# Chunk attention and an ELU feed-forward on one Trainium2 core: the middle group's second product by seven products of halves, and a new order of work

## The chip, the cores and the metric

One core of one Trainium2 chip runs the whole program as one launch. The metric is device time in microseconds (us). Three timed runs of the kernel before gave 825.3, 826.36 and 824.99 us (median 825.3). The profile is of one further execution, whose span from the first to the last instruction is 822.1 us.

## The reference

q, k and v are 8 x 8 x 576 x 64 in float32 (batch, heads, tokens, head size). Attention is local: every chunk of 64 tokens attends to itself.

```
scores = (q_c @ k_c.T) / 8          # per batch, head and chunk of 64 tokens
attn   = softmax(scores)
x      = attn @ v_c                 # laid out as 4608 tokens x 512
h      = x @ w_in                   # 512 -> 2048, the first product
g      = where(h > 0, h, exp(min(h, 0)) - 1)
out    = g @ w_out                  # 2048 -> 512, the second product
```

## The kernel before

**Numbers.** Each float32 operand of the two large products is held as a high and a low part ("hi", "lo"; a cast on ACT and a subtraction that makes the low part, together called a split below). One product of two tiles is three matmuls, hi.hi, hi.lo and lo.hi (`three`, L440), each 128x128 weights against 512 columns.

**Blocks.** The 4608 tokens are 9 blocks of 512. Blocks 0 to 2 are computed plainly: for each of 16 feature tiles f, `hidden` (L449) makes 12 matmuls of the first product, `elu` (L464) turns the result into g and splits it, and `second_products` makes 12 matmuls of the second product into four PSUM tiles `o0` to `o3`. The third block also prepares what the groups need.

**Groups.** Blocks 3 to 8 are three groups of two blocks (s = 0, 1, 2; s = 1 is the middle group). Their first product goes by Strassen-like combinations of halves: eight pairs of feature tiles a group, and for each pair seven products p1 to p7 of six matmuls (42 where the plain way needs 48). p1, p6, p7, p4 add up in one PSUM tile `x_ps`, p2, p5, p3 in another, `y_ps`; between them ACT copies intermediate sums out (`keep`, L764, items c1 to c4) and DVE adds them to the other tile (`add`, L767, items d1 to d3). A product that writes a tile next waits for the c or d that still reads it. `elu_of` (L685) then makes g of both blocks.

**Second product, groups 0 and 1.** g of the first block is multiplied at once, three matmuls for each of four token tiles (items Q; eight a pair, 24 matmuls). g of the other block is kept in `g_kept` and split (item G, `split_kept`, L818) and multiplied after the pairs (`KEPT`, 64 Q, 192 matmuls). The results are copied out and stored as rows of 512 features.

**Second product, group 2.** It goes by seven products of halves: products 1 and 2 in the course of the pairs (four Q a pair, 12 matmuls); then, in the order of `TURNED`, products 6, 5, 7, 4 and 3, each eight times 6 matmuls with the combination of weights as operand. `Pair.combine` (L743) makes the differences of g, `turn_split` (L1219) splits each operand into a ring of slots, `evacuate` (L1189) copies, adds, transposes and stores the transposed sums. Weight combinations come from DRAM: `combination` (L580) adds and subtracts parts of w_out on POOL, splits them and writes them to `b_dram`, half of the columns in group 0 (for two pairs in group 1's KEPT part) and half in group 1; `load_b` (L613) reads one back eight products ahead.

**Attention.** Each tile of 128 tokens is taken in ten steps, in blocks 3 on as letters: q k (DVE transposes, L365), s (scores on PE), m (maximum), E (exp), z (sums), h and w (normalise and transpose), v (times V on PE), x (copy out). One tile is done in every pair of groups 0 and 1 and one more in each KEPT.

**Order.** The engines run their instructions in program order, and the program order is written out by hand in strings of items: `START`, `FIRST_BLOCK`, `SECOND_BLOCK`, `LATER`, `THIRD_BLOCK`, `FIRST_PAIR`, `PAIR`, `LAST`, `TURNED`, `KEPT`. All loads but two and most stores are issued from SP's queue.

Of the kernel before, what the change touches and what calls it, by code (L numbers as in the profile page):

```python
# [21 lines left out]
def kernel(  # L22
# [19 lines left out]
    nc = tc.nc  # L42
# [18 lines left out]
    LAG = 1  # L61
    T2 = TB // 2
# [4 lines left out]

    first = ctx.enter_context(tc.tile_pool(name="first", bufs=1, side="right"))
# [4 lines left out]
    at = ctx.enter_context(tc.tile_pool(name="at", bufs=1))  # L73
    dram = ctx.enter_context(tc.tile_pool(name="dram", bufs=1, space=bass.MemoryType.DRAM))
# [16 lines left out]
    def w_out_tiles(pool):  # L91
        return [pool.tile([P, NF // 2, DM], F32R, name=name) for name in ("wo_hi", "wo_lo")]
# [81 lines left out]

    def subtract_next():
        (hi, lo), w = merged.pop(0)
        nc.vector.tensor_tensor(out=lo, in0=w, in1=hi.bitcast(F32), op=ALU.subtract)
# [97 lines left out]
    def early_attention(tt: int, q_sb, k_sb, get_v, kT, at, a_pool, get_banks, put, by_head: bool,  # L275
# [44 lines left out]
        else:  # L320
# [9 lines left out]
        nc.vector.tensor_tensor(  # L330
            out=a_heads, in0=a_heads, in1=z.broadcast_to([P, 2, NK, C]), op=ALU.mult
        )
# [15 lines left out]
    class Later:  # L348


        def __init__(self, n: int):
            self.n = n

# [19 lines left out]
        def less_max(self):  # L373
            mx = sm.tile([P, 2, NK, 1], F32, name="mx")
            nc.vector.tensor_reduce(out=mx, in_=self.scores, axis=AX.X, op=ALU.max)
            nc.vector.tensor_tensor(
                out=self.scores, in0=self.scores, in1=mx.broadcast_to([P, 2, NK, C]),
                op=ALU.subtract)

        def exp(self):  # L380
            nc.scalar.activation(out=self.scores, in_=self.scores, func=AF.Exp, scale=SCALE)

        def sums(self):
            self.z = sm.tile([P, 2, NK, 1], F32, name="z")
# [5 lines left out]
        def turn_a(self):  # L390

# [8 lines left out]

        def swap(self):

            for c in range(2):
                for e in range(2):
                    to, of = [slice(c * C + i * Q, c * C + (i + 1) * Q) for i in (e, 1 - e)]
                    nc.vector.transpose(
                        out=turned[to, 1 - e].rearrange("p (j h) t -> p j h t", j=2),
# [56 lines left out]
    def elu(h, engine=nc.vector):  # L464
# [13 lines left out]
        engine.tensor_tensor(out=glo, in0=e, in1=ghi.bitcast(F32), op=ALU.subtract)  # L478
# [25 lines left out]
    def combine():  # L504


        def pool(out, a, b, op):
            nc.gpsimd.tensor_tensor(out=out, in0=a, in1=b, op=op)
# [25 lines left out]
        def split(g):  # L534
            st = place_of(g)
            nc.scalar.copy(out=st[:, 0].bitcast(F32R), in_=st[:, 1])
            nc.vector.tensor_tensor(
                out=st[:, 1].bitcast(F32R), in0=st[:, 1], in1=st[:, 0], op=ALU.subtract)
# [41 lines left out]
    def combination(g: int, m: int, in_place: bool):  # L580

        half, f = divmod(2 * g, NF // 2)
        whi, wlo = [flat(w).bitcast(F32)[:, f * DM:(f + 2) * DM].rearrange(
            "p (i m c) -> p i m c", i=4, m=NM)[:, :, m] for w in (weights[half][2], weights[0][3])]
        sums = quad if in_place or g % 2 else k_turned
        a11, a21, a12, a22 = [sums[:, i] for i in range(4)]

        def pool(out, a, b, op):
            nc.gpsimd.tensor_tensor(out=out, in0=a, in1=b, op=op)

        pool(sums, whi, wlo, ALU.add)
# [7 lines left out]
        hi, lo = (spare(), flat(sums).bitcast(F32R)) if in_place else g_tiles()  # L599
        nc.scalar.copy(out=hi, in_=flat(sums))  # L600
        yield
        nc.vector.tensor_tensor(out=lo, in0=flat(sums), in1=hi.bitcast(F32), op=ALU.subtract)
        yield
        for i, src in enumerate((hi, lo)):
            nc.sync.dma_start(
                out=b_dram[g, :, 3:, i, m * P:(m + 1) * P],
                in_=src.bitcast(F32).rearrange("p (i c) -> p i c", i=4))
        yield
# [4 lines left out]
    def load_b(j: int):  # L613
        i, g = b_order[j]
# [723 lines left out]
```

## Time and profile before

| what | value |
|---|---|
| timed runs | 825.3, 826.36, 824.99 us, median 825.3 |
| span of the profiled execution | 822.1 us |
| PE busy | 814.1 us of the span, 5814 matmuls |
| DVE, ACT, POOL busy | 618.6, 492.4, 186.8 us |
| data moved | 181.40 MB, mean 221 GB/s |

A busy time is the sum over an engine's instructions. Matmuls overlap, so the time of one matmul in a row of them is read from the distance of starts, not from its own duration. Stages, in us from the span's start: the first product of block 0 starts at 27.5; block 1 at 125; block 2 at 218; the pairs of group 0 at 315, their KEPT part 442 to 487; the pairs of group 1 to 616.5, their KEPT part to 660; the pairs of group 2 to about 766, then the turned products until 818.5.

### The profile page before, as it was taken

To read this page: it belongs to the slowest core of one execution; us is meant where nothing else is said; L and a number is where in the kernel's file an instruction comes from. 1 tells how busy PE (TensorE), PEld (TensorE's weight loads), DVE (VectorE), ACT (ScalarE), POOL (GpSimd) and SP (SyncE) were. 2 spreads that over 40 slices of the span, in tenths; PEclk is the share of its full clock that TensorE was granted. 3 is DMA by queue.
4 is the path that set the end of the run, shared out by engine and by line. 5 is a ranking of instruction groups with operands and counts; after the bars stand their busy time and mean duration, and the time that the engine had idled before them with its cause. 6 is when DMAs were issued, how large, how long until landed. Compare 5 with 4: busy or idle time off the path is not lost.

```text
span 822.1 us, 15689 instructions
## 1 busy us (share of the span) xinstructions
PE 814.1 (99%) x5814; PEld 668.2 (81%) x5814; DVE 618.6 (75%) x947; ACT 492.4 (60%) x884; POOL 186.8 (23%) x196
## 2 busy tenths in 40 slices
PE   8999999999999999999999999999999999999998
PEld 7778788888888888888888888888888888888887
DVE  5999997777886798788778856778868547777745
ACT  6999985445644356665657336665566356777532
POOL 0000005554211210333343543234325000000000
PEclk9999999999999999999999999999999999999999
DMA  9947966776798996699999667899866357664677
GB/s 277 277 165 214 296 183 168 223 225 205 221 283 231 286 284 185 182 265 308 257 274 272 162 166 224 224 281 296 241 189 204 112 186 204 191 193 137 185 198 155
DMA packets 212075, 181.40 MB, mean 221 GB/s; under 512 B 73760, under 2 KB 190496, under 8 KB 212000
## 3 DMA queue, kind: packets, MB, share of 16 engines
q1 hardware_dynamic: 205088, 179.09, 77.6%
q10 hardware_dynamic: 6912, 1.31, 0.8%
q8 instruction: 46, 0.75, 0.4%
q14 instruction: 29, 0.24, 0.1%
HBM read 140.51 MB, written 42.99 MB: 223 GB/s over the span
## 4 chain that ended last, share of the span: by engine, by line
PE 97%; ACT 2%; DVE 0%; issue 0%; DVEq 0%; ACTq 0%
PE o L443 47%; PE h L443 43%; PE ps_a L259 2%; PE ps_a L267 2%; PE h L460 1%; ACT a L315 1%; PE ps_a L860 0%; PE ps_a L284 0%; PE ps_a L288 0%; PE ps_a L251 0%; PE ps_a L243 0%; ACT st L134 0%; ACT qT L340 0%; PE ps_a L335 0%; ACT xhi L434 0%; DVE mx L305 0%
## 5 line engine op out<-in xcount | busy, mean ns | idle before, releaser
L443 PE MATMUL o<-wo_hi,ghi 128*128 128x512 f32 x352 | 138.8, 394 | 0.0
L443 PE MATMUL o<-wo_hi,glo 128*128 128x512 f32 x352 | 137.4, 390 | 0.0
L443 PE MATMUL o<-wo_lo,ghi 128*128 128x512 f32 x352 | 137.1, 390 | 0.0
L443 PE MATMUL h<-xhi,wi_hi 128*128 128x512 f32 x324 | 108.1, 394 | 0.0
L443 PE MATMUL h<-xlo,wi_hi 128*128 128x512 f32 x324 | 106.7, 389 | 0.0
L700 POOL TENSOR_TENSOR glo<-e,ghi 128x512 fp32r<-128x512 f32 x32 | 41.4, 1293 | 172.1 <-ACT ghi L698 147.7
L443 PEld LDWEIGHTS o<-wo_hi,glo 128*128 128x128 f32 x352 | 66.1, 188 | 14.9 <-DVE glo L478 1.0
L443 PEld LDWEIGHTS o<-wo_hi,ghi 128*128 128x128 f32 x352 | 66.1, 188 | 14.0
L443 PEld LDWEIGHTS o<-wo_lo,ghi 128*128 128x128 f32 x352 | 66.1, 188 | 13.2
L443 PE MATMUL h<-wi_lo,wi_hi 128*128 128x512 f32 x288 | 75.0, 396 | 0.0
L765 ACT COPY kept<-h 128x512 f32<-128x512 f32 x72 | 42.1, 585 | 54.7 <-PE h L443 54.7
L443 PE MATMUL h<-wo_lo,wi_hi 128*128 128x512 f32 x288 | 71.8, 389 | 0.0
L443 PEld LDWEIGHTS h<-xhi,wi_hi 128*128 128x128 f32 x324 | 60.7, 188 | 13.3 <-ACT kept L765 0.4
L443 PE MATMUL o<-wo_hi,wo_lo 128*128 128x512 f32 x240 | 71.0, 390 | 0.0
L443 PEld LDWEIGHTS h<-xlo,wi_hi 128*128 128x128 f32 x324 | 60.8, 188 | 12.2
L443 PE MATMUL h<-xhi,wi_lo 128*128 128x512 f32 x180 | 70.2, 390 | 0.0
L443 PEld LDWEIGHTS h<-wo_lo,wi_hi 128*128 128x128 f32 x288 | 54.1, 188 | 11.2
L690 ACT ACTIVATE e<-e 128x512 f32<-128x512 f32 x96 | 60.8, 633 | 3.1
L443 PEld LDWEIGHTS h<-wi_lo,wi_hi 128*128 128x128 f32 x288 | 53.0, 188 | 11.4
L443 PE MATMUL o<-wo_lo 128*128 128x512 f32 (+1 forms) x198 | 60.2, 383 | 0.0
L693 DVE SCALAR_TENSOR_TENSOR g_kept<-e,g_kept 128x512 f32<-128x512 f32 x48 | 33.6, 701 | 31.5 <-ACT e L690 31.4
L467 ACT ACTIVATE e<-h 128x512 f32<-128x512 f32 x48 | 28.8, 600 | 41.5 <-PE h L443 38.0
(177 smaller groups left out, 1594.4 us busy)
## 6 DMA issues: line engine op xcount, KB each, us to landing
wi_hi<-a_dram SPq DMA_DIRECT2D x168, 256.0 KB, 4.1
wo_lo<-lo_dram SPq DMA_DIRECT2D x36, 512.0 KB, 5.5
wo_lo<-b_dram SPq DMA_DIRECT2D x56, 256.0 KB, 3.0
kept<-in_q_dram SPq DMA_DIRECT2D x100, 128.0 KB, 4.3
kept<-in_k_dram SPq DMA_DIRECT2D x100, 128.0 KB, 4.3
st<-in_moe_w_in_dram SPq DMA_DIRECT2D x16, 512.0 KB, 4.7
st<-in_moe_w_out_dram SPq DMA_DIRECT2D x16, 512.0 KB, 6.0
v_sb<-in_v_dram SPq DMA_DIRECT2D x32, 256.0 KB, 6.0
```

The lines of the kernel that those rows point to most:

```text
L259: nc.tensor.matmul(scores[halves[c], j, hp, :], lhsT=qT[halves[j], hp, halves[c]], rhs=kT[halves[j], hp, halves[c]], start=True, stop=True,)
L267: nc.tensor.matmul(x_ps[halves[j], c, hp, :], lhsT=v_sb[halves[c], 2 * hp + j, :], rhs=aT[halves[c], :, j * NK + hp], start=True, stop=True,)
L315: nc.scalar.activation(out=a_heads[:, j, h, :], in_=scores[:, j, h, :], func=AF.Exp, scale=SCALE, bias=mx[:, j, h, :], accum_out=z[:, j, h ...
L443: nc.tensor.matmul(ps, lhsT=a, rhs=b, start=start, stop=stop, skip_group_check=onto)
L460: nc.tensor.matmul(h, lhsT=w[:, kt, :], rhs=x[:, kt, :], start=i == 0, stop=i == len(terms) - 1)
L467: nc.scalar.activation(out=e, in_=h, func=AF.Relu, scale=-1.0)
L690: nc.scalar.activation(out=e, in_=e, func=AF.Exp, scale=-1.0)
L693: nc.vector.scalar_tensor_tensor(out=to, in0=e, scalar=-1.0, in1=c, op0=ALU.add, op1=ALU.max)
L700: engine.tensor_tensor(out=lo, in0=e, in1=hi.bitcast(F32), op=ALU.subtract)
L765: nc.scalar.copy(out=c21 if i == 4 else self.kept[i - 1], in_=x_ps)
```

## The change

The middle group's second product takes the seven products too (336 matmuls where it had 384). Its KEPT part goes; in its place stands `MID_TURNED`, with products 6, 5, 7, 4, 3, forty operand splits, the evacuations and the preparation of the last group's operands. Both column halves of every weight combination are now made in group 0 (`combination` has two tiles x and y). All strings behind `START` are written anew, with one string for each feature tile or pair. An item that ends in "!" has its two-input subtraction or addition moved to the other engine, from DVE to POOL or back (`combine_two`). Tile 28 takes its exponentials head by head, as six early tiles do (`BY_HEAD`). The high parts of w_out lie in pools of their own, and group 1's raw g, later its ring and group 2's `t2`, take their place.

```diff
+    def combine_two(engine, out, in0, in1, op=ALU.subtract):
+        if swapped[0]:
+            engine = nc.vector if engine is nc.gpsimd else nc.gpsimd
+        engine.tensor_tensor(out=out, in0=in0, in1=in1, op=op)
...
-    def combination(g: int, m: int, in_place: bool):
+    def combination(g: int, x, y, hx, hy):
...
+        pool(x, whi[:, :DM], wlo[:, :DM], ALU.add)
+        yield
+        pool(y, whi[:, DM:], wlo[:, DM:], ALU.add)
         yield
         pool(a22, a21, a22, ALU.add)
         pool(a21, a11, a21, ALU.subtract)
...
         def combine(self, item: str):
...
+            if s < NS - 1:
+                for to, a, b, op in {"1": [(b11, b12, b11, ALU.subtract)], "3": [(b12, b22, b12, ALU.subtract)],
+                                     "4": [(b21, b21, b22, ALU.subtract), (b21, b21, b11, ALU.add)]}[item]:
+                    combine_two(nc.gpsimd, to, a, b, op)
+                return
...
+    def turn_split(splits, ready, engine=nc.vector):
...
+            ring = ringed[-1] if n >= 2 * NG else weights[1][3]
+            hi, lo = [ring[:, 2 * (n % 4) + j, :] for j in range(2)]
+            if i == 6:
+                src = gp.tile([P, TB], F32, name="e")
+                combine_two(nc.vector, src, g_place(2 * g + 1), raw_place(0, g))
...
+            nc.scalar.copy(out=hi, in_=src)
+            combine_two(engine, lo, src, hi.bitcast(F32))
...
-    PAIR = (
-        "b b b m p1 c1 4 E Q 4 z p2 d1 Q p6 c2 b h b 1 Q Q 1 w p5 1 b q 1 Q l p7 c3 d2 k Q Q 2 p4 "
-        "c4 2 Q 3 p3 d3 3 3 3 s v x V"
+    MID_PAIRS = (
...
+        "p1 5 p2 c1 k p6 d1 5 4 4 E p5 c2 p7 c3 z h l d2 q w t1 Q 1 5 Q p4 t4 p3 c4 Q 2 s 1 1 "
+        "v 1 3 d3 2 Q x l t3",
...
+    MID_TURNED = (
+        "Y 6 H! 6 6 6 Y Y Q Z Q H Z G a10 a11 H! 6 6 s10 G! s11 5 t1! G 6 6 G 5 G t3! G G G! "
+        "5 u21 G 5 t4 5 G H G 5 5 5 u20 7 G! H! xB21 7 7 7 yB11! G! 7 G H! 7 G H! yt1! 7 xt3 "
+        "G G 7 u30 u31 4 4 xT1 H H! 4 G G! 4 H 4 a31 4 4 H G! G! a30 3 3 yt2! 4 s30 3 G 3 H! "
+        "G 3 yt4! s31 H! xT4 G! R 3 s40 xT2 R xT3! yB22 s41"
+    )
...
-        "s20 a21 s21 W1a s41a W0 s40 W1b s41b"
+        "4 G! a30 G 4 3 3 3 G! G! G! G! G s31 G! s30 3 3 3 3 G! G! G! G! 3 W1a W0 s41a a20 "
+        "s20 a21 s21 s40 W1b s41b"
...
-                (nc.scalar if which > 1 and i % 2 else nc.sync).dma_start(
+                (nc.scalar if which > 1 and i % 2 and s == NS - 1 else nc.sync).dma_start(
```

## Rows read from the trace of the kernel before

**Rows 1.** The page: busy time by engine; TensorE's granted clock in 40 slices.
```profile
PE 814.1 (99%) x5814; PEld 668.2 (81%) x5814; DVE 618.6 (75%) x947; ACT 492.4 (60%) x884; POOL 186.8 (23%) x196
...
PEclk9999999999999999999999999999999999999999
```

**Rows 2.** Busy time by stretch: stretch, length, PE, PEld, DVE, ACT, POOL, clock, DMA.
```profile
40.00:125.00 85.00, 85.00 (x603) 68.47 (x594) 78.81 (x115) 80.03 (x173) 0.00 (x0) 1.00 0.72 215
...
315.00:441.90 126.90, 126.90 (x968) 103.72 (x966) 101.31 (x165) 79.09 (x135) 40.05 (x45) 1.00 0.92 246
...
487.00:616.50 129.50, 129.50 (x1009) 105.97 (x1008) 94.42 (x155) 77.45 (x134) 46.95 (x55) 1.00 0.85 239
...
660.40:766.00 105.60, 105.60 (x467) 87.47 (x466) 72.19 (x111) 73.43 (x124) 0.00 (x0) 1.00 0.61 180
766.00:818.50 52.50, 52.48 (x248) 43.78 (x246) 32.00 (x51) 20.65 (x37) 0.00 (x0) 1.00 0.75 195
```

**Rows 3.** Waits of PE over the span, the longest group: total us, times, longest.
```profile
PE ps_a L243 <- ACT qT L340: 2.4, 3, 0.9
```

**Rows 4.** Timeline in group 2's pairs: start, us, engine, line, tiles, count, idle before.
```profile
696.87 1.52 PE L443 MATMUL h<-xhi,wi_hi 128*128 128x512 f32 x6
...
698.23 1.52 PE L443 MATMUL h<-xlo,wi_hi 128*128 128x512 f32 x6
...
698.43 0.59 ACT L765 COPY c<-h 128x512 f32<-128x512 f32 x1
...
699.59 1.52 PE L443 MATMUL h<-wi_lo,wi_hi 128*128 128x512 f32 x6
...
699.79 0.69 DVE L769 TENSOR_TENSOR g_kept<-h,kept 128x512 f32<-128x512 f32 x1 [0.71 <-PE h L443]
```

**Rows 5.** Group 1's pairs, DVE alone: tile ps_a; L365; L769; L693.
```profile
487.00:616.50 129.50, 8.81 (x480) 7.72 (x480) 39.59 (x77) 8.13 (x14) 1.00 0.85 239
...
487.00:616.50 129.50, 13.10 (x12) 1.00 0.85 239
...
487.00:616.50 129.50, 16.12 (x24) 1.00 0.85 239
...
487.00:616.50 129.50, 20.87 (x30) 1.00 0.85 239
```

**Rows 6.** Groups of instructions: forms, count, busy us, mean ns, idle before.
```profile
L700 POOL TENSOR_TENSOR glo<-e,ghi 128x512 fp32r<-128x512 f32 x32 | 41.4, 1293 | 172.1 <-ACT ghi L698 147.7 <-PE h L443 17.7 <-DMA kept<-in_k_dram 6.7
...
L683 DVE TENSOR_TENSOR xf<-xf 128x1024 f32<-128x1024 f32 x8 | 11.1, 1389 | 0.1
...
L678 DVE TENSOR_TENSOR wi_lo<-xf,wi_lo 128x1024 fp32r<-128x1024 f32 x6 | 7.7, 1279 | 0.0
...
L1226 DVE TENSOR_TENSOR wi_lo<-g_kept,wi_lo 128x512 fp32r<-128x512 f32 x8 | 5.3, 687 | 4.3 <-ACT wi_lo L1225 4.3
...
L1225 ACT CAST wi_lo<-g_kept 128x512 fp32r<-128x512 f32 x8 | 4.8, 622 | 7.2 <-issue 5.0 <-DVE wi_lo L1226 1.5 <-DVE wo_lo L1226 0.7
...
L1211 DVE STREAM_TRANSPOSE c<-o 128x512 f32<-128x512 f32 x3 | 2.1, 716 | 3.7 <-PE o L443 3.7
```

**Rows 7.** Timeline of DVE in group 1's KEPT part.
```profile
620.15 1.82 DVE L700 TENSOR_TENSOR wo_lo<-g_kept,wo_lo 128x512 fp32r<-128x512 f32 x2 [2.93 <-ACT wo_lo L698]
...
623.10 2.54 DVE L700 TENSOR_TENSOR wo_lo<-g_kept,wo_lo 128x512 fp32r<-128x512 f32 x2
```

**Rows 8.** Timeline of POOL over the same time.
```profile
620.64 2.74 POOL L589 TENSOR_TENSOR k_turned<-k_turned 128x128 f32<-128x128 f32 x4
623.35 1.74 POOL L589 TENSOR_TENSOR quad<-wo_hi,wo_lo 128x512 f32<-128x512 f32 x1
```

**Rows 9.** Line L700: duration in ns, least, median and most, first and last start.
```profile
L700 DVE TENSOR_TENSOR wo_lo<-g_kept,wo_lo x13: 678/693/1786, 445.1 to 644.5; 128x512 fp32r<-128x512 f32 x13
```

**Rows 10.** DMA issues: count, KB each, median us from issue to landing.
```profile
wo_lo<-b_dram SPq DMA_DIRECT2D x56, 256.0 KB, 3.0
```

**Rows 11.** Timeline near the end: two stores' issues on SP; the last DVE instruction.
```profile
800.63 0.87 SPq L1214 DMA_DIRECT2D out_dram<-k_turned  x2
...
818.51 0.45 DVE L1211 STREAM_TRANSPOSE c<-o 128x256 f32<-128x256 f32 x1 [1.43 <-PE o L443]
```

More of the change, by code (lines that the diff above doesn't have):

```diff
@@ L61 @@
     LAG = 1
+    TURN = 1
     T2 = TB // 2
@@ L1157 @@
     for f in range(NF):
-        for item in THIRD_BLOCK.get(f, ODD if f % 2 else EVEN).split():
+        for item in items_of(BLOCK_THREE[f]):
             if item == "H":
@@ L1205, in evacuate @@
             if which == 2:
-                to = (turned, unturned)[m].rearrange("p e h t -> p (e h t)")
-            elif which == 3:
+                to = spares[m]
+            elif which == 3 and s == NS - 1:
                 to = k_flat if m == 0 else flat(at.tile([P, NK, P], F32, name="qT"))
@@ L1264 @@
-            for item in order.split():
-                if item[0] == "u":
-                    evacuate(item)
+            order = (PAIRS, MID_PAIRS, LAST_PAIRS)[s][g]
+            if not s and 2 <= g < NG - 1:
+                combining = combination(g, *sum_places(g))
+            for item in items_of(order):
+                if item[0] in "uas" and len(item) > 1:
+                    evacuate(item, s)
+                elif item[0] in "AS" and len(item) > 1:
+                    evacuate(item.lower(), s - 1)
+                elif item in "GH":
+                    turn_split(splits, ready, nc.gpsimd if item == "H" else nc.vector)
@@ L1267 @@
                 elif not pair_step(item, before):
                     do(item)
-        if last:
-            break
+        if s >= TURN:
+            done = {i: 0 for i in range(1, 8)}
+            for item in items_of((MID_TURNED, TURNED)[last]):
+                if item in "65743":
+                    i, g = int(item), done[int(item)]
+                    done[i] += 1
+                    for m in range(NM):
+                        b_product(s, i, g, m, *(t2_place(g) if i == 6 and last else ready[i, g]))
+                elif item == "R":
+                    for m in range(NM):
+                        queue.append((s, 3, done[3], m, *ready[3, done[3]]))
+                    done[3] += 1
+                elif item[0] == "W":
+                    for g in range(done[4], NG):
+                        b_product(s, 4, g, int(item[1]), *ready[4, g],
+                                  {"a": slice(T2), "b": slice(T2, TB)}.get(item[2:], slice(TB)))
+                elif item in "GH":
+                    turn_split(splits, ready, nc.gpsimd if item == "H" else nc.vector)
+                elif item == "Q":
+                    second_next()
+                elif item in "YZ":
+                    next(pair.parts["3" if item == "Y" else "4"])
+                elif item[0] in "uas":
+                    evacuate(item, s)
+                elif item[0] == "t":
+                    pair.combine(item[1])
+                else:
+                    do(item)
+            continue
@@ L1273 @@
         for row, line in enumerate(KEPT):
-            if s == NS - 2 and row == 0:
-                combining = chain(combination(0, 0, False), combination(1, 0, False))
-            for item in line.split():
+            if row == 0:
+                combining = chain(*[combination(g, *sum_places(g)) for g in (0, 1, NG - 1)])
+            for item in items_of(line):
                 if item == "4":
```

330 lines of the change are left out of this document (192 added, 138 removed), and 111 rows, old and new, of tables (BLOCK_THREE, BLOCK_TWO, FIRST_BLOCK, KEPT).

## The prediction

> **What bounds the kernel now.** I read the page's busy times first, then the stretches, then the waits of TensorE (PE), and last the timeline at a few places. PE is busy for 814.1 of 822.1 us, and its granted clock stands at the top digit in all 40 slices [rows 1]. In every stretch from 40 us on PE's busy time is the stretch itself (126.90 of 126.90, 129.50 of 129.50, 105.60 of 105.60) [rows 2]. A busy PE could still step slowly, so the step has to be read: six matmuls of 512 columns start 1.36 us after the six before them (696.87, 698.23, 699.59), which is 0.2267 us each [rows 4]. PE's longest group of waits is 2.4 us in all [rows 3], and since PE is busy without a gap behind 40 us, it lies in the start. So from 27.5 us to the last matmul the time is the number of matmuls times their step, and only two things can change it: fewer matmuls, or waits that aren't there today.
>
> The other engines are below PE: DVE 101.3 of 126.9 in group 0's pairs (80%), 94.4 of 129.5 in group 1's (73%), 72.2 of 105.6 in group 2's [rows 2].
>
> **What is removed.** The middle group's second product takes 2 blocks x 16 feature tiles x 4 token tiles x 3 = 384 matmuls. By seven products it takes 7 x 8 pairs x 2 column halves x 3 = 336, 96 of them for products 1 and 2 in the pairs and 240 for the other five behind them. 48 matmuls go, 48 x 0.2267 = 10.9 us [rows 4]. All have 512 columns, as the ones that go. I counted the other matmuls in the strings: first products, attention tiles and the number of changes between large and small matmuls (16 in block 0, four in block 1) are as before. The start string is the same, so the first large matmul stays at 27.5 us.
>
> **What is added beside PE, middle group's pairs.** The stretch now holds 38 Q where it had 64, so 26 x 3 x 0.2267 = 17.7 us less: 129.5 - 17.7 = 111.8 us. DVE's work in it today is attention 39.6 + 13.1, the additions d1 to d3 16.1, and ELU's last step 20.9 [rows 5]; 94.4 less these leaves 4.7 for the weight combinations' splits, which move to group 0. New on DVE are 13 subtractions that "!" puts there, 13 x 0.687 = 8.9 [rows 6]. Sum: 39.6 + 13.1 + 16.1 + 20.9 + 8.9 = 98.6 of 111.8 us, 88%. POOL has 12 splits, 20 differences of g and 4 parts of the first turned operands, 36 x 1.293 = 46.5 us [rows 6]. ACT loses eight casts (8 x 0.622 = 5.0): 72.5 of 111.8 [rows 2, 6]. Tile 28's exponentials head by head turn one ACT instruction into sixteen short ones, in one pair; the third of ACT that is free covers them.
>
> **Turned part of the middle group.** 38 products of 6 and two Q: 234 matmuls, 53.0 us, against 192 matmuls (43.5) in the part that goes. DVE: 24 low parts and 7 other subtractions at 0.687 (21.3), four additions at about 0.69 (2.8), six transposes at 0.716 (4.3), and for the last group's operands five of 1.279 and four of 1.389 (12.0): 40.4 of 53.0 us, 76% [rows 6]. ACT: 37 casts at 0.622 (23.0), seven of twice the size, at most twice that (8.7), and eight copies and ELU steps, estimated at a cast each (5.0): 36.7 of 53. POOL: 18 x 1.293 and two of twice the size, 28.5 us. All are under PE. They need an order in which each comes in time, and group 2 has such an order today: PE 52.48 of 52.50 us with DVE at 61% [rows 2].
>
> **Group 0.** Its pairs keep their length. On DVE come four more splits of combinations (2.7) and about seven moved subtractions and additions more than leave (4.8), from 101.3 to about 109 of 126.9; with a few transferred preparations at most 112, 88%. POOL goes from 40 to about 50. Each combination now writes 1 MB in the group where it wrote half of that: 5 x 0.5 MB more in 127 us on a mean of 246 GB/s, 8% more traffic [rows 2]. The loads of operands are issued a whole pair (16 us) ahead, so I take nothing for it.
>
> **SP's queue.** The middle group's stores all go through SP now: 32 at 0.44 us each [rows 11], 14 us of issue in 53, in order with 40 weight loads. A weight load is issued eight products ahead (8 x 1.36 = 10.9 us) and lands 3.0 us after issue [rows 10], so a store that waits for its transpose may hold it back by some 7 us before PE sees it. Cost: nothing; if a transpose came over 7 us late, what it is late by.
>
> **Moved in block 0 to 2 and in the last group.** No PE wait is there to be won, so there is nothing below zero; what hides the new order is that block 0 runs without a PE wait at DVE 78.8 and ACT 80.0 of 85.0 us [rows 2]. In the tail two pairs of stores fall behind the product of whole columns instead of ahead of it; the last instruction is the same half transpose [rows 11]: 0 to +1 us, I take 0.
>
> **Waits that the new order may add.** Today c copies are covered by one product (1.36 us) in group 2, and d additions by at least 2.04 (p, Q). By my count of the new strings 15 of 69 hand-offs through DVE are left with one product. ACT's copy and DVE's addition both start 0.20 us after the last matmul's successor has started and take 0.59 and 0.69 [rows 4]; a covered d has 1.36 - 0.89 = 0.47 us to spare. An instruction of DVE ahead of it takes up to 1.09 (13.10 over 12) [rows 5], so the worst is 0.62 late, 15 x 0.62 = 9.3 us; the least is 0, as in block 0. Behind a late d stands PE's next product, and PE has nothing else. The nearest row is block 0, with DVE at 93% and no wait, so I take 1.0 us, keep 0 and 9.3 for the range.
>
> **The sum.** 822.1 - 10.9 + 1.0 = 812.2 us of span. The runs' median lies 3.2 us above the profiled span, which I carry over: **815.4 us**.
>
> **A shared way to memory.** POOL and DVE disturb each other: two DVE subtractions with both inputs in SBUF took 1.82 us beside POOL's additions, two more 2.54 [rows 7, 8], where the median is 0.693 and the most 1.786 [rows 9]. That is 4.36 - 4 x 0.69 = 1.6 us over for four, 0.40 each. The change puts POOL to work all through the group. The Trainium skill (SBUF — State Buffer, "Who interferes with whom") says that a VectorE instruction with two SBUF inputs and a GpSimd instruction that reads SBUF exclude each other for the whole instruction. The rows agree with it in kind; the sum by it would be rival A's, 819.
>
> **Rivals.**
>
> A: in the turned part POOL's instructions and DVE's with two SBUF inputs run one at a time. Two-input work in it is 21.3 + 12.0 = 33.3 us on DVE and 28.5 on POOL, 61.8 in 53.0. Two double-sized POOL subtractions (5.2) may run on below the last group's first pair: 56.6, 3.6 us over: 815.4 + 3.6 = 819.0. For it: rows 7 and 9. Against it: in group 1's KEPT part PE lost nothing to these; part of each instruction may overlap, and the first splits run ahead.
>
> B: the hand-offs cost their worst, 9.3 instead of 1.0: 823.7, no change to be measured. Against it: DVE would have to be behind each time.
>
> C, slower: DVE becomes the bound of the pairs. If each two-input subtraction or ELU step there waits for POOL: 43 in the middle pairs, some 45 in group 0's, 39 in the turned part. DVE's room is 111.8 - 98.6 = 13.2, 15 and 12.6 us. At a mean delay p the overrun is 127p - 41 us: nothing below 0.32 us, 9.8 us at 0.40, and over the gain and the bound of measurement (10.9 + 1.7) from 0.42 on. At 0.45, 16.2 us: 814.4 + 16.2 = 830.6. For it: 0.40 for four instructions in the rows. Against it: these all met POOL, and POOL is busy 42% of the middle pairs, which makes a mean nearer to 0.2.
>
> D: the matmuls aren't saved. The strings hold 336, so I give it nothing.
>
> **Numbers.** What a measurement here can tell from no change is 0.2%, 1.7 us. Forecast (813.2 to 817.5) 0.70; A and its like (up to 821.5) 0.16; B 0.06; C 0.08. The forecast and A are faster, B is the same, C slower: 0.86, 0.06, 0.08. The range 813.2 to 821.5 holds the first two.
>
> **What would show it.** PE with 5766 matmuls, busy in all of every stretch behind 27.5 us; the middle pairs 112 us long with DVE near 99, the turned part 53. A PE wait on an addition of L767's kind would show B; subtractions of over 1 us beside POOL, and PE waiting on low parts in the turned part, A; the same in the pairs, with DVE at the stretch's length, C. The forecast is wrong if PE's waits behind 27.5 us sum to more than 3 us.

## The result, and the profile after

The changed kernel takes 831.5 us (median of 4 runs, 830.4 to 833.1) against 825.5 beside it: ratio 1.0074, 95% interval 1.0060 to 1.0089. It is slower, where 815.4 was forecast and 821.5 was the end of the range. The profiled execution took 833.1 us, the longest of the four, and its span is 831.3. So the places below account for the 9.2 us between two profiled spans, where the medians differ by 6.0.

First the page of the changed kernel, for [rows 1]: busy time, TensorE's granted clock, the traffic, and the chain that ended last.
```profile
PE 811.3 (98%) x5766; PEld 660.3 (79%) x5766; DVE 628.1 (76%) x917; ACT 507.1 (61%) x925; POOL 348.6 (42%) x267
...
PEclk9999999999999999999999999999999999999999
...
DMA packets 225390, 187.72 MB, mean 226 GB/s; under 512 B 91168, under 2 KB 199712, under 8 KB 225312
...
PE 81%; DVE 8%; ACT 5%; DMA 3%; issue 2%; SPq 1%; POOL 0%; DVEq 0%; ACTq 0%; POOLq 0%
```
The chain on the page before:
```profile
PE 97%; ACT 2%; DVE 0%; issue 0%; DVEq 0%; ACTq 0%
```
The 48 matmuls are gone (5766 for 5814). POOL has nearly twice its work. In the chain 19% is now something other than PE's work; before it was 3%.

The stretches, for [rows 2] (same columns): block 0, group 0's pairs, the middle pairs, the turned part, the last pairs, the tail.
```profile
40.00:125.00 85.00, 83.27 (x551) 65.97 (x549) 77.35 (x92) 76.89 (x168) 31.43 (x20) 1.00 0.73 214
316.10:443.00 126.90, 126.71 (x908) 103.56 (x908) 104.72 (x168) 79.14 (x136) 49.89 (x43) 1.00 0.89 251
493.70:615.60 121.90, 115.01 (x929) 91.82 (x928) 100.17 (x160) 77.96 (x136) 57.77 (x41) 0.99 0.82 230
615.60:670.40 54.80, 54.41 (x237) 44.02 (x236) 43.46 (x52) 32.27 (x52) 24.69 (x17) 1.00 0.75 200
670.40:776.00 105.60, 104.53 (x460) 85.79 (x459) 66.39 (x92) 72.17 (x126) 37.02 (x25) 1.00 0.67 187
776.00:827.50 51.50, 51.49 (x243) 43.02 (x241) 22.30 (x29) 20.32 (x35) 29.28 (x21) 1.00 0.78 194
```
The middle pairs take 121.9 us, not 111.8, with DVE at 100.2 (82%), not far from the 98.6 forecast: the work was counted rightly, the time wasn't. PE stands still for 6.9 us in them and for 1.7 in block 0, where it had stood for none.

The waits of PE behind its first large matmul: us in total, times, longest.
```profile
PE h L492 <- DVE c L835: 2.8, 3, 2.4
PE h L492 <- DMA wi_hi<-a_dram: 2.5, 1, 2.5
PE h L492 <- ACT kept L831: 1.2, 2, 0.9
PE h L492 <- DVE e L519: 1.1, 1, 1.1
PE ps_a L279 <- DVE turned L455: 1.0, 1, 1.0
PE o L492 <- DVE kept L532: 0.8, 1, 0.8
```
No single cause stands out in this view, and the engine named is the last in a row of causes. I took all starts of large matmuls and added up what each came later than its step of 0.2267 us: 16.8 us behind the first large matmul, where it was 0.16 before. By place: blocks 0 to 2 2.8, group 0 and KEPT 3.2 (with 0.9 at 496.8 and 498.3 us, where KEPT's last products alternate with the first middle pair), middle pairs 8.5, turned part 0.9, last pairs 1.4. The sum of the span: 822.1 - 10.9 + 16.8 - 0.2 + 1.1 (the first large matmul starts at 28.6, not 27.5) + 2.2 (single steps longer by up to 0.12 us, and 0.4 near the end) is 831.1, and 831.3 was measured.

**The two longest waits go back to SP.** SP's issues and the matmul that waited, in the middle pairs:
```profile
514.60 5.98 SPq L243 DMA_DIRECT2D kept<-in_q_dram  x8
...
520.62 5.32 SPq L243 DMA_DIRECT2D kept<-in_k_dram  x8
...
526.04 1.83 SPq L705 DMA_DIRECT2D wi_hi<-a_dram  x3
...
529.39 2.98 PE L492 MATMUL h<-wo_lo,wi_hi 128*128 128x512 f32 x12 [2.49 <-DMA wi_hi<-a_dram]
```
Tile 31 lies across two batches and needs sixteen loads. SP issues them in one row for 11.3 us; the weight operand of product 6 stands behind them, is issued at 526.04 at the earliest and comes 2.5 us late. Before, the same sixteen went out in one row too, with no wait of PE:
```profile
513.21 4.19 SPq L223 DMA_DIRECT2D kept<-in_q_dram  x8
517.44 4.83 SPq L223 DMA_DIRECT2D kept<-in_k_dram  x8
522.37 1.18 SPq L643 DMA_DIRECT2D wi_hi<-a_dram  x2
```
So it isn't the row by itself that costs, but how soon PE needs what stands behind it. Some 30 us on, the same queue is late for tile 33:
```profile
551.56 1.97 SPq L243 DMA_DIRECT2D kept<-in_q_dram  x4
...
558.34 1.08 DVE L384 STREAM_TRANSPOSE qT<-kept 128x512 f32<-128x512 f32 x1 [4.04 <-DMA kept<-in_q_dram]
...
561.18 0.68 DVE L835 TENSOR_TENSOR c<-h,kept 128x512 f32<-128x512 f32 x1
...
561.91 2.06 PE L492 MATMUL h<-wo_lo,wi_hi 128*128 128x512 f32 x6 [2.36 <-DVE c L835]
...
563.77 2.75 PE L492 MATMUL h<-t_place,wi_hi 128*128 128x512 f32 x6
```
The wait is put down to DVE, but DVE had itself waited 4.04 us for q of tile 33, whose load SP issued only at 551.56, with the pair's first sum queued behind. Six matmuls then take 2.75 us where they took 1.52: in 562.2 to 566.3 us the granted clock is 0.59, near the lower level (1.2 of 2.4 GHz), after a PE that had stood still for 2.4 us. By the steps that adds 1.6 us to the 2.5.

The operands of the second product land later as well, here in 500 to 612 us, for [rows 10], whose median was 3.0 us (all 56 of those loads were the last group's, so the place differs too):
```profile
wo_lo<-b_dram SPq DMA_DIRECT2D x18, 256.0 KB, 4.8
```

**Block 0.** DVE, POOL and PE around the first wait:
```profile
36.60 1.69 DVE L162 TENSOR_SCALAR st<-st 128x1024 f32<-128x1024 f32 x1
...
37.70 1.74 POOL L193 TENSOR_TENSOR wi_lo<-xf,wi_hi 128x512 fp32r<-128x512 f32 x1
38.21 1.78 DVE L193 TENSOR_TENSOR wo_lo<-xf,wo_hi 128x512 fp32r<-128x512 f32 x1
...
42.58 0.50 PE L492 MATMUL h<-xhi,wi_hi 128*128 128x512 f32 x1 [1.07 <-DVE e L519]
```
A subtraction of 0.69 us takes 1.78 beside POOL's, and what stands behind it on DVE comes late for PE. Over the whole run DVE's longer instructions take some 50 us more than the medians of their forms, against some 10 before; 16 of these lie in the first 125 us, where before had 0.2.

**The last pairs.** The first sum into c waits for the middle group's stores out of c:
```profile
677.07 0.69 DVE L835 TENSOR_TENSOR c<-h,kept 128x512 f32<-128x512 f32 x1 [2.06 <-DMA out_dram<-c]
```

### The profile page after: what moved, and what is told of

It is laid out like the page before. It is cut to its first block, busy times and chain, and to the rows that moved or that the text cites. A ratio compares the mean times of both kernels' runs of the same rounds, so it can differ in the third digit from the quotient of the medians.

```text
span 831.3 us, 15888 instructions
## 1 busy us (share of the span) xinstructions
PE 811.3 (98%) x5766; PEld 660.3 (79%) x5766; DVE 628.1 (76%) x917; ACT 507.1 (61%) x925; POOL 348.6 (42%) x267
## 4 chain that ended last, share of the span: by engine, by line
PE 81%; DVE 8%; ACT 5%; DMA 3%; issue 2%; SPq 1%; POOL 0%; DVEq 0%; ACTq 0%; POOLq 0%
PE o L492 39%; PE h L492 36%; PE ps_a L279 2%; PE ps_a L287 1%; DMA wi_hi<-a_dram 1%; ACT st L140 1%; DVE wo_lo L193 1%; ACT st L145 1%; DVE xf L169 1%; DMA b_dram<-unturned 1%; PE h L509 1%; DMA kept<-in_q_dram 1%; ACT a L335 1%; DVE xf L173 1%; DVE turned L455 1%
## 5 line engine op out<-in xcount | busy, mean ns | idle before, releaser
L193 POOL TENSOR_TENSOR glo<-e,ghi 128x512 fp32r<-128x512 f32 x36 | 49.6, 1377 | 156.4 <-ACT ghi L524 111.8
L492 PE MATMUL o<-wo_hi,ghi 128*128 128x512 f32 x272 | 107.7, 396 | 0.0
L492 PE MATMUL o<-wo_hi,glo 128*128 128x512 f32 x272 | 106.3, 391 | 0.2 <-POOL glo L193 0.2
L492 PE MATMUL o<-wo_lo,ghi 128*128 128x512 f32 x272 | 106.0, 390 | 0.0
L492 PE MATMUL h<-wi_lo,wi_hi 128*128 128x512 f32 x288 | 70.3, 391 | 0.0
L492 PEld LDWEIGHTS o<-wo_hi,glo 128*128 128x128 f32 x272 | 51.1, 188 | 12.0 <-DVE glo L193 0.7
L492 PEld LDWEIGHTS o<-wo_hi,ghi 128*128 128x128 f32 x272 | 51.1, 188 | 11.0 <-ACT ghi L524 0.2
L492 PEld LDWEIGHTS o<-wo_lo,ghi 128*128 128x128 f32 x272 | 51.1, 188 | 10.2
L835 DVE TENSOR_TENSOR g_kept<-h,kept 128x512 f32<-128x512 f32 x48 | 33.1, 689 | 27.2 <-PE h L492 14.5
L492 PEld LDWEIGHTS o<-wo_lo 128*128 128x128 f32 x246 | 45.4, 188 | 10.3 <-DVE wo_lo L193 0.6
```

Of the source, the lines that this page charges most:

```text
L193: engine.tensor_tensor(out=out, in0=in0, in1=in1, op=op)
L492: nc.tensor.matmul(ps, lhsT=a, rhs=b, start=start, stop=stop, skip_group_check=onto)
L835: nc.vector.tensor_tensor(out=to, in0=y_ps, in1=self.kept[kept], op=ALU.add)
```

## The experiments

Each time stands beside the kernel before, 825.3 to 825.5 us in all sets.

| run | us | ratio to before, 95% |
|---|---|---|
| e1 old blocks | 831.6 | 1.0040 to 1.0116 |
| e2 no swaps | 861.9 | 1.0434 to 1.0468 |
| e3 loads moved | 828.3 | 1.0026 to 1.0060 |
| e4 POOL in before | 830.9 | 1.0055 to 1.0085 |
| e5 repaired | 827.2 | 1.0013 to 1.0035 |
| e6 new blocks | 829.3 | 1.0039 to 1.0062 |
| e8 spread | 828.0 | 1.0022 to 1.0049 |
| e9 quarter loads | 825.7 | 0.9999 to 1.0018 |
| e10 no turns | 827.6 | 1.0012 to 1.0039 |
| e11 best | 825.9 | 0.9993 to 1.0010 |
| e12 two queues | 832.5 | 1.0063 to 1.0121 |
| e13 places | 825.7 | 0.9996 to 1.0014 |
| e14 KEPT's end | 828.3 | 1.0020 to 1.0043 |
| e15 first block | 822.3 | 0.9946 to 0.9973 |

My theory after the result: the matmuls are saved in full, and the loss lies at single places with causes of their own (POOL beside DVE in block 0, SP's order, the stores out of c). The rival: DVE, at 88% of the middle pairs by the forecast, has no slack left, so that what is repaired in one place is paid for in the next.

**e1, blocks 0 to 2 as before**
```diff
-    FIRST_BLOCK, BLOCK_TWO, BLOCK_THREE of the changed kernel
+    FIRST_BLOCK, SECOND_BLOCK, LATER, THIRD_BLOCK of the kernel before
```


> The changed kernel with the orders of blocks 0, 1 and 2 as they were before (27 to 315 us of the trace). The changed kernel's PE waits in block 0 sum to 2.6 us, and its first large matmul starts 1.1 us later than before. If the new order of block 0 makes them (with 22 subtractions moved to POOL), both go: 831.5 - 2.6 to - 3.7, 828 to 829 us, and PE has no wait behind 28 us until 430 us. If PE's waits there are the chip's or memory placement's, the time stays within 1 us of 831.5. Either way the waits from 430 us on stay, some 14 us.

831.6 us, no gain. Block 0's waits are gone, but PE now waits 2.7 us at 321.5 us, with slow matmuls behind, in group 0's first pair: the older third block leaves ScalarE another backlog than the new pair was ordered for. What the blocks cost stayed open.

**e2, every "!" without effect**
```diff
-            swapped[0] = item[-1] == "!"
+            swapped[0] = False
```


> The changed kernel with every '!' without effect: each subtraction stays on the engine that it had. Theory 'shared reading' (POOL's instructions and DVE's with two SBUF inputs wait for each other): DVE's lengthened instructions in block 0, KEPT and the turned parts fall from 52 us in all to under 25, PE's waits in block 0 (2.6 us) and in KEPT (2.9 us) go, and the time falls by 3 to 6 us, to 825.5 to 828.5. Rival 'DVE is full': with 22 subtractions back on DVE in block 0 and a dozen in KEPT, DVE is late and the time rises, over 832. Theory 'SP's queue' expects the waits at 526 to 529 us and 559 to 566 us, some 6.5 us together with the slower clock behind them, to stay in either case.

861.9 us: PE's waits sum to 43 us. A "!" moves operations both ways (net, 51 more run on POOL with them: 267 instructions there, 216 without), and the rest of the order is built on it. So this run can't price POOL beside DVE; it shows that this order is worse without the moves.

**e3, tile 31's loads in two halves, tile 33's earlier**
```diff
-        ... "p4 1 c4 1 V 3 1 m p3 d3"          "p1 p2 5 E c1 l z 4 ... p7 Q Q 4 t1 ..."
+        ... "p4 1 c4 1 V 3 1 m p3 d3 j"        "p1 p2 5 E c1 z 4 ... p7 Q Q J 4 t1 ..."
-        ... "Q m 3 1! Q"                       "... c3 z h l d2 q w t1 ..."
+        ... "Q m 3 1! Q l"                     "... c3 z h d2 q w t1 ..."
```
(j issues tile 31's q, J its k.)

> The changed kernel with three loads of tokens moved in SP's queue, nothing else: tile 31's sixteen loads in two halves, eight at the end of the first middle pair and eight behind p7 of the second (were: sixteen together ahead of p6's operand of the next pair), and tile 33's eight at the end of the third middle pair (were: behind p7's operand in the fourth). Theory 'SP's queue': the wait of 2.5 us on p6's operand at 529 us and the wait of DVE (4.0 us) on tile 33 with PE's 2.4 us and the stretch at half clock behind it go: 831.5 - 5 to - 7, 824.5 to 826.5 us, granted clock back to 1.000 in most runs. Rival 'DVE is the bound of the middle pairs' (88% and waits): PE waits as long for DVE elsewhere in the same stretch, and the time stays over 829.

828.3 us, 3.2 less in the median and 6.6 in the profiled executions. The matmul that had waited 2.49 us for its operand, from the trace of this run:
```profile
526.47 1.65 PE L492 MATMUL h<-wo_lo,wi_hi 128*128 128x512 f32 x6 [0.15 <-DVE c L835]
```
The wait at 561.9 and the half clock are gone too; a new wait of 2.0 us comes at 534.7, where DVE turns tile 31's k before it has landed. SP's order is shown as a cause.

**e4, the kernel before with POOL in block 0**
```diff
-        nc.vector.tensor_tensor(
+        (nc.gpsimd if on_pool else nc.vector).tensor_tensor(
```
(22 of the first block's subtractions, those that the new string marks; nothing else differs from before.)

> The kernel before, in its own order, with 22 of block 0's subtractions on POOL, those that '!' marks in the changed kernel (13 low parts of weights, 9 of g). Theory 'shared reading': DVE's own work falls by 15 us but its instructions are lengthened by 8 us or more in block 0, POOL's subtractions are late, and PE, which had no wait there, gets waits of 1 to 6 us: 826.5 to 831.5. Rival 'only the new order costs': an engine with less work and the same order makes no wait: 825.5, within 0.5 us.

830.9 us, 5.6 slower by these moves alone. One of them, from its trace:
```profile
46.15 1.73 POOL L181 TENSOR_TENSOR wi_lo<-xf,wi_hi 128x512 fp32r<-128x512 f32 x1
46.66 2.37 DVE L181 TENSOR_TENSOR wo_lo<-xf,wo_hi 128x512 fp32r<-128x512 f32 x2
...
48.48 0.50 PE L447 MATMUL o<-wo_lo,ghi 128*128 128x512 f32 x1 [0.75 <-DVE wo_lo L181]
```
Two subtractions that remain on DVE take 2.37 us where they need 1.4, and PE waits for the second. Giving DVE less to do made DVE later.

**e7, the shared reading by itself**
```diff
+    for beside in (None, act, gp_two):
+        for on_vector in (vector_two, vector_bank, vector_one, vector_three, vector_turn):
+            barrier()
+            for i in range(12):
+                on_vector()
+                if beside and (beside is act or i < 6):
+                    beside()
```


> The shared reading measured by itself; no part of the computation is done. VectorE runs twelve instructions of one kind on 128x512 float32, five kinds in turn (subtraction of two SBUF tiles, of a PSUM and an SBUF tile, scalar addition of one SBUF tile, the scalar_tensor_tensor of two SBUF tiles, the transpose); first alone, then beside twelve ScalarE copies, then beside six GpSimd subtractions of two SBUF tiles; then six GpSimd subtractions run alone. Theory (VectorE and GpSimd read SBUF in turns, instruction by instruction): alone 0.69 us each (transpose 1.1); beside ScalarE the same; beside GpSimd a VectorE instruction that meets one takes 1.0 to 1.8 us, and the stretch of twelve is longer by 4 to 6 us, for the kinds with two SBUF inputs, and for the scalar addition too; the transpose and the one with a PSUM input less. Rival (only kinds with two SBUF inputs take turns): scalar addition, PSUM subtraction and transpose unchanged to within 5%.

Its timeline: start, us for all instructions of the row, engine, line, tiles, count. First VectorE alone (two SBUF inputs, scalar addition), then beside six GpSimd subtractions (two SBUF inputs, PSUM and SBUF, scalar addition, transpose), last GpSimd alone.
```profile
9.13 8.68 DVE L45 TENSOR_TENSOR dv<-a,b 128x512 f32<-128x512 f32 x12
...
28.59 5.50 DVE L60 TENSOR_SCALAR dv<-a 128x512 f32<-128x512 f32 x12
...
102.16 9.60 POOL L45 TENSOR_TENSOR po<-c,d 128x512 f32<-128x512 f32 x6 [0.31 <-ACT ac L50]
102.32 14.34 DVE L45 TENSOR_TENSOR dv<-a,b 128x512 f32<-128x512 f32 x12
...
117.65 8.67 DVE L45 TENSOR_TENSOR dv<-bank,b 128x512 f32<-128x512 f32 x12
...
127.30 11.17 DVE L60 TENSOR_SCALAR dv<-a 128x512 f32<-128x512 f32 x12
...
154.80 8.92 DVE L66 STREAM_TRANSPOSE dv<-a 128x512 f32<-128x512 f32 x12
...
164.55 7.96 POOL L45 TENSOR_TENSOR po<-c,d 128x512 f32<-128x512 f32 x6 [0.31 <-ACT ac L50]
```
Each GpSimd subtraction takes 0.94 us from VectorE ((14.34 - 8.68) / 6, and (11.17 - 5.50) / 6 for the scalar addition), and beside the two-input kind loses 0.27 itself ((9.60 - 7.96) / 6). With one input in PSUM (8.67) and in the transpose (8.92, as alone) nothing is lost, nor beside ScalarE. A subtraction costs VectorE 0.72 us: moved to GpSimd beside work of the first kinds, it costs VectorE more than if it had stayed. My theory held: 5.7 us more for twelve, where 4 to 6 were expected. Where I had expected less, at the PSUM and transpose kinds, there was nothing; alone, the scalar addition took 0.46 us and the transpose 0.74, not 0.69 and 1.1. The rival was wrong on the scalar addition. The Trainium skill (SBUF — State Buffer, "Who interferes with whom") says that VectorE and GpSimd exclude each other where VectorE has two SBUF inputs or runs a copy or scalar operation in one of its modes that use both ports, and not with one SBUF input otherwise; all five kinds agree, the scalar addition if it runs in such a mode, which the trace doesn't name. The amount is less than a full exclusion would make it: one after the other the subtractions would have taken 8.68 + 7.96 = 16.6 us, and 14.34 was measured.

**e5, repairs together, and e6, the same with the new blocks.** e5 is e1 and e3 with the middle group's stores s30, s31 from other buffers and three items moved; e6 leaves the blocks and group 0's first pair as in the changed kernel.
```diff
-            elif which == 3 and s == NS - 1:
+            elif which == 3:
```


> The changed kernel with four repairs: blocks 0 to 2 in the order of before, tile 31's and tile 33's loads moved ahead as in the run before, the stores s30 and s31 of the middle group from k_flat and qT in place of c11 and c21 (so that the last group's first sum needn't wait for them), and three orders changed inside pairs (group 0's first pair copies its first product ahead of the operand's last split; tile 31's k is turned one product later; one second product goes from ahead of p4 to behind p3 in the sixth middle pair). Theory: the lost time lay in these few places and the 48 matmuls are saved in full (10.9 us). TensorE's waits behind the first large matmul then sum to 3 to 5 us instead of 16.8, none is over 1.1 us, no stretch is at the half clock, and the time is 819 to 822 us. Rival (VectorE, at 88% in the middle pairs, sets the end there by itself): waits of 1 us and more turn up again elsewhere between 500 and 665 us, their sum in that stretch stays over 4 us, and the time is 825 us or more.

> The same as the kernel of the run before it in this set, but blocks 0 to 2 in the new order (and group 0's first pair as in the changed kernel). The difference of the two prices the new order of the blocks by itself, which the first run left unsettled because a wait of 2.7 us at group 0's start took its place. Theory (the subtractions moved to GpSimd lengthen VectorE's own, and TensorE waits in block 0): 2.6 to 4 us slower than the other, 823 to 826 us, with TensorE waits of 2.5 us or more between 40 and 110 us. Rival (the blocks cost nothing, as the prediction had it): within 1 us of the other.

827.2 and 829.3 us. The blocks' new order costs 2.1 us by this, close to the 2.8 of its waits: the rival for e6 falls. The difference rather understates the blocks, since e5 alone starts 1.2 us late in group 0's first pair, where its two orders meet. e6 is also e3 with the stores and two moves added, and no faster (829.3 and 828.3 us, intervals overlapping): these repairs brought nothing that can be measured. For e5 the rival's number came true, over 7 us of waits between 500 and 665 us; but the largest (3.46) ended on an operand's load behind token loads on SP again, not on VectorE. The stores were the wrong ones: the last group's first sum waited 4.23 us for s40 and s41.

**e8, token loads one at a time; e9, a quarter of them; e10, without the small transposes**
```diff
+                beat[0] += 1
+                if later_loads and beat[0] % 2 == 0:
+                    issue_next()
-                to = (c11, c21)[m]
+                to = (c11, c21)[m] if s == NS - 1 or which != 4 else (k_flat, flat(...))[m]
```
(e9: `if spread and (j or half): continue`. e10: `for c in range(0 if self.n > PLAIN * NTT + 17 else 2)`.)

> The changed kernel with blocks 0 to 2 in the order of before and the places repaired where TensorE still waited in the repaired kernel: in the middle pairs the token loads are no longer issued eight or sixteen in a row, but one at a time, between every second item of the order, so that no operand's load stands behind more than one of them; the middle group's last stores (s40, s41) leave from k_flat and qT, since there the last group's first sum waited 4.23 us for the stores out of c; group 0's first pair keeps the older place of its first eviction, the last rows of KEPT and the seventh middle pair have one item moved each. Theory (SP's queue, with its issues of 0.5 to 0.6 us in one order, is what is left of the loss in the middle pairs; the DMA wait of 3.3 us at 553 us was its last sign): no TensorE wait for an operand's load is over 0.5 us, the waits behind the first large matmul sum to 3 to 6 us, and the time is 818 to 823 us, below before. Rival (VectorE in the middle pairs): the waits on loads go but waits on VectorE of as much come, their sum between 500 and 665 us stays over 4 us, and the time is 825 us or more.

> The kernel of the run before it with only one of every four token loads (q and k) of tiles 31 to 35 issued; the attention of these tiles is then computed on what the buffers held, so this part is left out of the result. SP's issues fall by some 36 (0.5 to 0.6 us each) and the traffic by some 2.3 MB. Theory (with the loads spread out SP no longer sets anything): within 1 us of the kernel before it. If SP's queue or the DMA traffic still cost time there: 2 us or more faster, and TensorE waits between 500 and 615 us that end on loads are gone.

> The kernel of the first run of this set without the four small transposes of VectorE (1.82 us together) for each of tiles 30 to 35, so the crossed quarters of these tiles' scores are left out. VectorE has some 11 us less in the middle pairs (about 87 of 112 us in place of 98). Rival (VectorE at 88% sets the end of the middle pairs): the waits on VectorE there go and it is 2 us or more faster than the first of this set. Theory (single places, not VectorE's fullness): within 1.2 us of it (the one wait for the turned scores before the seventh pair's end, 1.0 us, may go).

e8, 828.0 us: no wait on a load over 0.8 us is left and none on stores, but an edit of mine in group 0's first pair brought a new one. Its trace:
```profile
325.71 2.36 POOL L193 TENSOR_TENSOR xlo<-xf,xlo 128x1024 fp32r<-128x1024 f32 x1 [13.68 <-ACT xlo L750]
...
326.00 2.62 DVE L765 SCALAR_TENSOR_TENSOR e<-e,c 128x512 f32<-128x512 f32 x1
...
329.81 1.75 PE L503 MATMUL h<-xhi,wi_hi 128*128 128x512 f32 x4 [3.12 <-ACT kept L842]
```
One GpSimd subtraction of double size holds an ELU step of VectorE (0.69 us) for 2.62; ScalarE's conversion and copy stand behind it, and PE waits 3.1 us (what the subtraction has to do with that, e11 tells).

e10 is 0.4 us faster than e8, with 11 us less for VectorE: within the intervals. By the starts of the large matmuls its middle pairs take 116.7 us, e8's 118.4. VectorE's fullness falls as the main explanation; a part of up to 1.7 us isn't excluded. e9 is 2.3 us faster: the token loads still cost that much, as issues or as traffic.

**e11, two orders changed, and e12, half of the spread loads issued by ScalarE**
```diff
-        ... m xB22! 1 1 q c3 d2 Q 1 E 2        ... p3 Q h 2 w d3 s 2 v c4 3 Q
+        ... m xB22 1 1 q c3 d2 Q 1 E 2         ... p3 Q h 2 w d3 Q s 2 v c4 3
-        nc.sync.dma_start(out=to, in_=of)
+        (nc.scalar if beat[1] % 2 else nc.sync).dma_start(out=to, in_=of)
```
(the last two lines are e12's)

> The kernel with the token loads spread out, with two edits: in group 0's first pair the subtraction of 128x1024 for B22, which ran on GpSimd beside one scalar_tensor_tensor of VectorE (2.62 us where it takes 0.69) and made TensorE wait 3.28 us at 329.8 us, goes back to VectorE; in the seventh middle pair one second product of TensorE is put ahead of the attention's scores, which waited 1.0 us for the turned weights. Theory (one GpSimd instruction beside a chain of one product's cover is enough for that wait and the half clock behind it): the wait at 329 us and the slow matmuls behind it go, 4 to 5 us, and with the wait at 596 us the time is 822 to 824 us, below before. Rival (the time lost in one place turns up at the next, since VectorE has no slack): 826 us or more.

> The kernel of the run before it, with every second of the spread token loads of tiles 31 to 35 issued by ScalarE in place of SP (some 24 issues). With a quarter of these loads issued the time was 2.3 us less. If that was SP's queue (its issues of 0.5 to 0.6 us ahead of operand loads): 1 to 2 us faster than the kernel before it, or less by what ScalarE's issues delay its evictions. If it was the traffic: the same within 0.5 us. If ScalarE's own order suffers (an issue stands ahead of an eviction that TensorE waits for, or waits itself for VectorE's reads of the buffer): 1 us slower or more, with new TensorE waits on ScalarE between 530 and 600 us.

e11, 825.9 us, level with before: the long ELU step is 0.69 again, yet PE still waits 2.3 us there, since ScalarE's copy stands behind the same conversion. So the subtraction was the smaller part of that wait. e12 is 6.6 us slower, the third case. PE's waits on ScalarE in it, 3.0 us in e11:
```profile
PE h L504 <- ACT kept L843: 9.2, 6, 2.3
```
One of ScalarE's issues, and the copy behind it, for which PE waited 1.76 us:
```profile
521.09 0.34 ACTq L374 DMA_DIRECT2D kept<-in_k_dram  x1
521.47 0.59 ACT L843 COPY kept<-h 128x512 f32<-128x512 f32 x1 [0.85 <-DMA kept<-in_q_dram]
```
So e9's 2.3 us isn't split into queue and traffic.

**e13, that copy ahead of the conversion and tile 33's q turned later; e14, one conversion from KEPT's end into the first middle pair**
```diff
-        c2 xT4 1 p5 p7 m xB22 1 1 q c3 d2 ...     "p1 q c1 4 p2 5 Q m E d1 V p6 p5 5 c2 ..."
+        c2 xT4 1 p5 p7 c3 d2 m xB22 1 1 q ...     "p1 c1 4 p2 5 Q m E d1 V p6 p5 5 q c2 ..."
-        xT4! b! b Q xB22! G!                      "p2 p1 c1 d1 Q Q 1 p6 ..."
+        xT4! b! b Q G!                            "p2 p1 c1 d1 xB22! Q Q 1 p6 ..."
```
(the last pair of lines is e14's)

> The kernel that stood level with before (825.9 us), with two orders changed. Its two largest waits: 2.48 us at 327.8 us, where ScalarE's copy of the fifth product (needed before the next can overwrite its bank) stood behind the conversion of an activation that VectorE gave late, and slow matmuls behind it; and 1.4 us at 557 us, where VectorE's turn of tile 33's q waited 2.92 us for its load with the pair's first sum behind it. The copy goes ahead of that conversion, the turn of q behind the pair's fourth product. Theory (each wait is one place's order, and VectorE has slack enough between them): both go, no new one of over 1 us comes, and the time is 821 to 823.5 us, faster than before by more than 0.2%. Rival (VectorE, 88% busy there, has no slack: what is saved in one place is waited for at the next): 825 us or more.

> The kernel of the run before it, with one conversion and its subtraction (128x1024 each, for B22) moved from the end of KEPT into the first middle pair, behind that pair's first sums: at 496.7 us TensorE waited 0.85 us for ScalarE's copy of the first product, which stood behind two such conversions. Theory: 0.5 to 1 us faster than the kernel of the run before it. Rival (the 128x1024 subtraction on GpSimd now lies beside VectorE's first sums of the pair and lengthens them): the same or slower by up to 3 us, with a wait on VectorE between 500 and 512 us.

e13 stayed at 825.7: the wait at 557 went, the one at 328 became two of 1.9 and 0.8 at the next conversion. By its number the rival wins; but the place is again the mixed first pair. e14, 828.3: KEPT's wait went, but in its profile VectorE waits 3.9 us for a token load at 526.6. That load isn't what was moved, so e14 tells nothing certain of the move.

**e15, before's order in the first block alone**
```diff
-    FIRST_BLOCK of the changed kernel
+    FIRST_BLOCK of the kernel before
     (BLOCK_TWO, BLOCK_THREE and PAIRS as changed; loads, stores and KEPT's first row as in e8, middle pairs as in e13)
```


> The changed kernel with the order of before in its first block alone (blocks 1 and 2 and group 0 in the new order, so that the wait of 2 to 3.3 us in group 0's first pair, which came with the mixture of the older third block and the new pair, cannot be there), the token loads of the middle pairs spread out, the middle group's last stores from other buffers, and the small moves of single items in KEPT and in the third, fifth and seventh middle pairs. Theory (the loss lies at single places, each with its own cause: GpSimd beside VectorE in the first block, SP's order in the middle pairs, the stores of the last group): TensorE's waits behind the first large matmul sum to 4 to 6 us, none over 1.1 us, no slow stretch, and the time is 820 to 823.5 us, faster than before by more than 0.2%. Rival (VectorE has no slack, a repaired place is paid for at the next): 825 us or more again.

822.3 us (12 runs), 3.1 less than before and 9 less than the changed kernel: the theory's number. Its page, block 0 and the middle pairs (the same matmuls as in the row of the changed kernel), and PE's longest waits; the profiled execution, 824.7 us, is the second longest of the twelve:
```profile
PE 809.4 (98%) x5766; PEld 659.3 (80%) x5766; DVE 628.9 (76%) x940; ACT 506.4 (62%) x925; POOL 313.5 (38%) x244
```
```profile
40.00:125.00 85.00, 84.97 (x619) 68.09 (x619) 77.78 (x114) 79.26 (x172) 0.00 (x0) 1.00 0.70 215
488.70:608.80 120.10, 116.07 (x929) 91.57 (x928) 101.15 (x160) 77.55 (x135) 58.23 (x41) 0.99 0.90 233
```
```profile
PE h L503 <- DMA wi_hi<-a_dram: 2.1, 1, 2.1
PE h L503 <- DVE g_kept L846: 0.4, 1, 0.4
```
Block 0 has no wait. The middle pairs take 120.1 us for 121.9, with DVE as busy as before the repair. By the large matmuls' starts the 8.4 us between the two profiled executions come from block 0 (2.7), the last pairs (1.7), the middle pairs (1.7), KEPT (1.2), the start (0.6) and group 0's pairs (0.5). Late starts sum to 8.9 us, more than I had expected (4 to 6), with one of 2.2 on a load at 567 us and slow matmuls behind it. So the number came, but the middle pairs are not repaired in this trace: by the same starts they are shortest in e9, with 116.0 us, where 111.8 was forecast.

## Why the prediction was wrong

**Matmuls.** Right: 48 fewer, at an unchanged step; the sum above closes with all 10.9 us.

**SP's queue and the loads, "cost: nothing".** Wrong, and the largest error: 6.7 us in the profiled execution (2.65 + 2.52, and 1.57 at the lower clock), and 3.2 in the median by e3. I weighed the 32 stores of the turned part, behind which no weight load came late for PE, and took the weight loads of the pairs as a whole pair ahead. What I didn't count was the token loads in the same queue at their new places: sixteen in a row ahead of product 6's operand, and tile 33's behind product 7's. The kernel before issues the same sixteen without a wait, so their place had to be read against the new order.

**Block 0 to 2, "what hides the new order".** Wrong by 2.8 us in the trace and 2.1 by e5 and e6. I read DVE at 78.8 of 85 us as cover and priced a move to POOL as relief. Rows 7 to 9 had the price, 0.40 us for each DVE instruction in them and 1.786 us at most. I used it in the rivals alone, for the turned part (A, where 0.9 us was lost, not 3.6) and the groups (C), and in the forecast and for block 0 not at all; there e4 measured 5.6 us for such moves alone, in the order of before.

**Waits that the new order may add, 1.0 us.** The range of 0 to 9.3 held what was left: 16.8 less 6.7 and 2.8 is 7.3 us, for which I had 1.0: 3.2 in group 0 and KEPT, 1.8 at evictions and turned weights of the middle pairs, 0.9 in the turned part, and 1.4 at the last group's first sum. The last is no hand-off of PE and DVE but a buffer that a store still reads, which I had not named; e8 moved the stores, and the wait went.

**Rival C** named 830.6 us, and 831.5 came, but not by its mechanism: its sign was DVE at the length of the pairs, and DVE has 100.2 of 121.9 us there; e10 took 11 us of VectorE's work away with little effect, and e15 took 9 us off with VectorE as busy. That the number fits is luck. D falls with 5766 matmuls; B's late sums are there, though mostly behind loads.

The mark that I had set, waits of more than 3 us behind 27.5 us, is met five times over. Open: what keeps the middle pairs at 116 us and more in every run; how e9's 2.3 us divide into queue and traffic; why runs of e15 lie between 819.9 and 826.2 us, where before's lie within 3.5 us; and the 1.1 us by which the first large matmul started later in this one trace (27.8 to 28.8 us in the others, e4's included, which keeps before's order).

## What to carry to other kernels

A queue that issues in order has to be read at the place where each load stands, with all that it carries: a load "a pair ahead" is late if sixteen others go first. Moving an operation to an engine that shares a way to memory with the busy one can cost the busy one more than it gives, so the price is taken beside the work that it will meet. And a schedule at 99% of one engine has no average slack: check each place that moves, and expect a hand-made mixture of two good orders to have a wait at the seam.

## What the runs showed of the hardware that I had not expected

Of the 24 starts of large matmuls that came 1.8 us late or more in these traces, 17 were followed by five to eight matmuls at about half rate, such as the stretch with a granted clock of 0.59 above (1.6 us more for a wait of 2.5); after seven, the one at 529.4 us among them, the clock stayed at 1.00. So a long wait is to be priced by what follows it, too; what decides between the two cases these traces don't show. GpSimd's subtraction takes 0.94 us from VectorE's scalar addition as well, though that has one SBUF input (e7). ScalarE as a second queue made things worse (e12, 6.6 us): its issues stand in one order with its copies, and PE's waits on these rose from 3.0 to 9.2 us. In the 0.85 us ahead of the copy at 521.47 ScalarE ran nothing but one issue of 0.34; what held that issue isn't shown.
